# Attention and feed-forward on one core: the value products of two head pairs put into one TensorE step

## The chip, the cores and the metric

The kernel runs on one core of one Trainium2 chip. The metric is the device time of one execution in microseconds (us). Engines are named as the profile names them: PE is TensorE's matmuls, PEld its weight loads, DVE is VectorE, ACT is ScalarE, POOL is GpSimd, SP issues the DMAs. [...]

## What is computed

Attention over a window of 128 keys and 4 sink keys, for 4 sequences of 768 tokens with 8 heads of 64, and then a feed-forward product with a squared ReLU:

```python
keep = is_sink | in_window
scores = np.where(keep, scale * q @ k.T, -1e9)
a = np.exp(scores - max(scores))
a = a / (sum(a) + 1e-9)
x = a @ v                          # put together as 3072 tokens x 512
out = np.maximum(x @ w_in, 0) ** 2 @ w_out    # w_in 512 x 2048, w_out 2048 x 512
```

All is float32. The products of the feed-forward part are made exact enough by splitting both factors into a high and a low part, so that each product takes three matmuls.

## The kernel before

The 3072 tokens are eight chunks of 384 (half a sequence each). A chunk's attention goes by four head pairs (two heads of 64 fill the 128 partitions), so there are 32 pair steps `s` in all. A chunk's feed-forward part goes over 16 slices `fc` of 128 of the 2048 columns. For each slice PE makes the first product (line 837, 12 matmuls of 384 columns), ACT takes ReLU and square (850, 854), DVE makes the exact square's low part (859, 866), and one slice later PE makes the second product (882, 9 matmuls of 512 columns).

One pair of attention goes through these steps, from the third chunk on (`s >= 8`):

- scores on PE (521), two matmuls over KS and QS, which hold high and low parts that ACT, DVE or POOL have made (388, 478, 484, 489);
- mask and maximum on DVE (498), exponential on ACT (504), sum's reciprocal on DVE (562), and scaling of P by it, on POOL (569; in the first two chunks also on DVE, or on ACT in line 567);
- P is turned by DVE in blocks of 32 x 32 into T (727, 731); four DMAs put T into `via` in DRAM (744) and one DMA gets it back as PT with whole columns turned (757);
- the four sink columns of P are copied into the tile PSK in a high part (585) and a low part (583), both by POOL. DVE turns PSK into SKT (647), four small DMAs gather it (653), and ACT or DVE copies it to SK (388);
- the value step on PE: for each block of keys and each head a matmul of 64 columns of v against PT (785), which uses half of the array's columns, both heads side by side; then one matmul over the full array for the sinks (789). ACT and DVE then split the sum into x's high and low part (801, 806).

In the first two chunks (`turned`) PE itself turns P (698) and the sink columns (630), and scores are made from kn and qn with 64 rows of the array (515).

Which instruction stands where in each engine's queue is decided before the program runs, by the class `Plan`. Each step has a rank, the engines that may do it with an assumed cost, and the cells that it reads and writes. `Plan.order` picks step by step the one that could start first by these costs. Its numbers are the planner's, not the chip's. Three of its rules matter here: a step marked "port" (an SBUF pass of DVE or POOL) is not put beside another such pass of the other engine; a POOL step without that mark waits for `SHARE` of the running DVE pass; and a change of PE's mode (0: the full array, 1: 64 rows, 2: 64 columns) is priced at 0.2 each time. All engines then work through their queues in order.

In SBUF, many tiles share a place: PT is one buffer for all pairs, T is one buffer for both heads of a pair, PSK has two, and the ReLU's result r has two (G0 and G1). Three PSUM banks ("att") serve scores and value sums from the second chunk on.

Of the kernel before, what the change touches and what calls it, by code (L numbers as in the profile page):

```python
# [18 lines left out]
P = 128  # L19
D = 64  # L20
NS = 4
# [12 lines left out]
SHARE = 0.5  # L34
# [4 lines left out]
SC_DVE = 0.3  # L39
CLAIM = (True, False)  # L40
KS_ACT = 0.0
URGE = 0.5
LOW_DVE = 0.0
CP_DVE = 0.3
SC_ACT = 0.3
# [8 lines left out]
def f32(ap):  # L54
    return ap.bitcast(F32)


class Plan:
# [45 lines left out]
    def order(self):  # L104
# [3 lines left out]
        while open_:  # L108
# [16 lines left out]
            for e, able in best.items():  # L125
# [5 lines left out]
                if chosen is None or a[0] < chosen[1][0] or (e == "POOL" and a[0] <= chosen[1][0] + 0.001):  # L131
                    chosen = e, a
# [37 lines left out]
def sink_window_attention_moe(  # L170
# [25 lines left out]
    with ExitStack() as fast:  # L196
# [18 lines left out]
        ident = wp.tile([P, P], F32, name="ident")  # L215
# [39 lines left out]
        either = sb("G1", [P, P], F32, "either")  # L255
# [16 lines left out]
        PSK = [wp.tile([P, NQ, 32], F32R, name=f"PSK{i}") for i in range(2)]  # L272
# [3 lines left out]
        for t in (VS, PSKW, *PSK, *SK):  # L276
            nc.gpsimd.memset(f32(t), 0.0)
# [6 lines left out]
        PT = wp.tile([P, 4, 2 * NQ, 2, 32], F32, name="PT")  # L284
        PT_flat = PT.rearrange("p r i h b -> p (r i h b)")
# [126 lines left out]
        def attention(s, rank):  # L412
# [36 lines left out]
            if plain:  # L449
                which = (0, 1, 2, 0, 2, 0, 2, 0)[s]  # L450
                if which == 1:
                    both = lambda: sb("T", [P, 2, NQ, BAND], F32, f"P_{s}")
# [121 lines left out]
            psk = PSK[two]  # L574
            psk_cell = ("PSK", two)
            if turned:
                psk = PSKW[:, two]

            def part_sinks(h, low):
                src = Pt(h)[:, i0:NQ, P:BS]  # L580
                to = psk[:, i0:NQ, 0 : 6 * NS].rearrange("p q (t c) -> p q t c", c=2 * NS)[..., h * NS : h * NS + NS]
                if low:
                    nc.gpsimd.tensor_tensor(to[:, :, 1], src, f32(to[:, :, 0]), op=ALU.subtract)
                else:
                    nc.gpsimd.tensor_copy(to[:, :, 0:3:2], src.unsqueeze(2).broadcast_to([P, NQ - i0, 2, NS]))  # L585

            groups = ((0, 1),) if plain else ((0,), (1,))
            for heads in groups:
# [10 lines left out]
                for h in heads:  # L599
                    for i in range(NQ):  # L600
# [12 lines left out]
                        ("POOL", 0.2), r - URGE + 0.01, lambda h=h: part_sinks(h, False),  # L613
# [3 lines left out]
                        ("POOL", 0.2), r - URGE + 0.01, lambda h=h: part_sinks(h, True),  # L617
# [8 lines left out]
            if turned:  # L626

                def turn_sinks():
# [5 lines left out]
                    ("PE", 0.11 * (NQ - i0), 0), r, turn_sinks, reads=own_sinks + [("spare", 23)], writes=[key], take=[("any" if early else "att", key)],  # L634
# [9 lines left out]
            else:  # L644
# [13 lines left out]
                for x in range(4):  # L658
# [3 lines left out]
                add(  # L662
                    [("ACT", 0.4), ("DVE", 0.35, "port", CP_DVE)], rank(0.8) - URGE,
                    lambda e: copy(e, sk[0:32, :, i0:NQ], rows_()[0:32, :, i0:NQ]),
                    reads=VR, writes=[sk_cell],
                )
# [3 lines left out]
            if turned:  # L670
# [6 lines left out]
                for bi, members in enumerate(parts):  # L677
# [15 lines left out]
                    def turn(blocks=blocks, key_t=key_t):  # L693
# [12 lines left out]
                        reads=[(P_cell(h), i) for h in hs for i in range(NQ)] + [P_cell(h) for h in hs],  # L706
# [8 lines left out]
            else:  # L715
                T = lambda: sb("T", [P, 4, 2 * NQ, 2, 32], F32, f"T_{s}")
                used = 2 * NQ - i0

                def turn(h, which):
                    if which == 0:  # L720
                        dst, src = T()[:, :, 0:NQ, h], Pt(h)[:, :, BS:BAND]
                    elif which == 1:
                        dst, src = T()[:, :, NQ : 2 * NQ - 1, h], Pt(h)[:, 1:NQ, 0:P]
                    else:
                        dst, src = T()[:, :, 2 * NQ - 1, h], Pt(h)[:, 0, 0:P]
# [6 lines left out]

                for h in range(2):
                    r = rank(1.3 if not plain and h == 0 else 0.9)
                    for which in range(3 - i0):
                        add(
                            ("DVE", (0.49, 0.33, 0.2)[which]), r - URGE, lambda h=h, which=which: turn(h, which),
                            reads=[(P_cell(h), i) for i in range(NQ)] + [P_cell(h)] + ["T"] * (h + which > 0),
                            writes=[("T", h, which)] + ["T", ("TP", 0), ("TP", 1)] * (h + which == 0),
                        )  # L740
                via = lambda: dram(f"via{s % 2}", [4, 32, 4, 2 * NQ, 2, 32], f"via_{s}")

                def put(r):
                    nc.sync.dma_start(
                        out=via()[:, :, r, 0:used].rearrange("c a i h b -> a c (i h b)"),
# [473 lines left out]
```

## Time and profile before

| | |
|---|---|
| median of the runs shown | 678.01 us (676.47, 678.01 and 1077.74) |
| the profiled execution's own time | 677.97 us |
| its span, first to last instruction | 676.2 us |
| granted TensorE clock over the span | 0.994 |
| DMA | 104.91 MB in 62547 packets, mean 155 GB/s |

The span is what the views show; 1.8 us of the execution's time lie outside of it. In the views, a row "L785 PE MATMUL bank<-PT,vn" is the matmul of line 785 that reads PT and v and writes a bank; "x12" counts its records (a float32 matmul in the 64-column form leaves two). The chain of work goes back from the last instruction to what released it, so that its pieces fill the span without gaps: the length of a PE piece there is the time until the next piece, not the time for which one matmul is under way. Behind an arrow stands what ended an engine's idle time.

### The profile page before, as it was taken

The page shows a single profiled execution, that of the slowest core. Times are in us where ns is not written, and L with a number is a line of the kernel's source. Part 1 is how long each engine was busy: PE and PEld are TensorE (multiplying, and loading weights), DVE is VectorE, ACT ScalarE, POOL GpSimd, SP SyncE. Part 2 cuts the span into 40 slices and gives each one's busy share as a digit, 9 for nine tenths or more (in the row PEclk, how much of TensorE's full clock was granted, in tenths as well). Part 3 has the DMA queues.
Part 4 walks back from the last instruction along what each step waited for, and adds up shares of the span by engine and source line. Part 5 has one row for each costly group of instructions (what it writes and reads, how often), then busy time and mean ns, then how long its engine had stood idle before and what let it go on. Part 6 is the DMA issues. An engine that isn't in the chain of part 4 may idle for free.

```text
span 676.2 us, 11302 instructions
## 1 busy us (share of the span) xinstructions
PE 658.2 (97%) x3662; PEld 573.3 (85%) x3662; DVE 445.5 (66%) x1211; ACT 392.5 (58%) x1142; POOL 125.2 (19%) x319
## 2 busy tenths in 40 slices
PE   4999999999999999999999999999999999999996
PEld 3767889998888888898888888888889888899985
DVE  7899999878877656575667756665666664242221
ACT  5898644367665445566666676666677665542221
POOL 4542200033242221111112211111121221000000
PEclk9899999999999999999999999999999999999999
DMA  7856665025977544366555856557556853310001
GB/s 235 261 155 187 208 207 177 32 75 165 263 200 205 165 120 121 109 209 198 176 158 170 243 168 192 175 164 200 164 157 187 245 169 118 115 62 1 1 0 52
DMA packets 62547, 104.91 MB, mean 155 GB/s; under 512 B 10800, under 2 KB 39216, under 8 KB 62480
## 3 DMA queue, kind: packets, MB, share of 16 engines
q1 hardware_dynamic: 62480, 104.11, 51.8%
q8 instruction: 31, 0.51, 0.3%
q14 instruction: 36, 0.29, 0.1%
HBM read 78.72 MB, written 24.38 MB: 152 GB/s over the span
## 4 chain that ended last, share of the span: by engine, by line
PE 89%; DVE 7%; POOL 1%; issue 1%; DMA 1%; ACT 0%; SPq 0%; DVEq 0%; POOLq 0%
PE bank L882 39%; PE bank L837 38%; PE bank L785 5%; PE bank L521 5%; DVE P L498 2%; PE bank L789 1%; DVE w L350 1%; DVE f L333 1%; DVE f L340 1%; DVE f L326 1%; DVE P L569 1%; DMA kn<-in_k_dram 1%; POOL PSK_wide L585 1%; DVE gl L866 0%; PE bank L515 0%
## 5 line engine op out<-in xcount | busy, mean ns | idle before, releaser
L837 PE MATMUL bank<-x,w 128*128 128x384 f32 x1536 | 301.2, 338 | 0.0
L837 PEld LDWEIGHTS bank<-x,w 128*128 128x128 f32 x1536 | 266.1, 188 | 8.3 <-issue 1.4
L882 PE MATMUL bank<-w,gh 128*128 128x512 f32 x768 | 242.6, 397 | 0.0
L569 POOL TENSOR_SCALAR P<-P,small 128x260 f32<-128x260 f32 (+1 forms) x168 | 83.4, 513 | 415.6 <-DVE small L562 401.2
L882 PEld LDWEIGHTS bank<-w,gh 128*128 128x128 f32 x768 | 138.7, 188 | 22.4 <-issue 1.0
L882 PE MATMUL bank<-w,gl 128*128 128x512 f32 x384 | 151.8, 395 | 0.0
L850 ACT ACTIVATE r<-bank 128x384 f32<-128x384 f32 x128 | 62.7, 490 | 114.1 <-PE bank L837 112.8
L504 ACT ACTIVATE P<-P,nbs 128x260 f32<-128x260 f32 (+1 forms) x192 | 93.6, 488 | 60.3 <-DVE nbs L498 57.9
L859 DVE TENSOR_TENSOR bank<-bank,r 128x384 f32<-128x384 f32 x128 | 72.0, 563 | 77.4 <-ACT r L850 76.8
L498 DVE CUSTOM_DVE_ANT_0 P<-bank,maskA 128x260 f32<-128x260 f32 x128 | 53.1, 421 | 53.4 <-PE bank L521 52.8
L882 PEld LDWEIGHTS bank<-w,gl 128*128 128x128 f32 x384 | 72.1, 188 | 16.9
L866 DVE TENSOR_TENSOR gl<-bank,gh 128x384 fp32r<-128x384 f32 x128 | 71.1, 556 | 19.1 <-ACT gh L854 10.1
L854 ACT ACTIVATE gh<-r 128x384 fp32r<-128x384 f32 x128 | 66.7, 521 | 2.8 <-PE bank L882 0.7
L727 DVE STREAM_TRANSPOSE T<-P 128x384 f32<-128x384 f32 x96 | 45.3, 494 | 24.8 <-POOL P L569 24.7
L521 PEld LDWEIGHTS bank<-KS,QS 128*128 128x128 f32 x288 | 52.0, 188 | 5.7
L521 PE MATMUL bank<-KS,QS 128*128 128x260 f32 (+1 forms) x288 | 54.8, 277 | 0.0
L785 PE MATMUL bank<-PT,vn 128*64 128x256 f32 (+1 forms) x392 | 40.6, 347 | 0.0
L801 ACT CAST x<-bank 128x384 fp32r<-128x384 f32 x32 | 15.2, 474 | 42.1 <-PE bank L789 42.1
L785 PEld LDWEIGHTS bank<-PT,vn 128*64 128x64 f32 x392 | 25.7, 139 | 15.7 <-issue 6.3
L504 ACT ACTIVATION_READ_ACCUMULATOR P<-P,nbs 128x1 f32 x192 | 36.0, 188 | 0.0
L498 DVE CUSTOM_DVE_ANT_0 P<-bank,mask 128x128 f32<-128x128 f32 (+1 forms) x64 | 22.0, 353 | 19.3 <-PE bank L521 19.0
L374 ACT ACTIVATE sq<-sq,theta 128x256 bf16<-128x256 bf16 x64 | 32.2, 503 | 1.1
(99 smaller groups left out, 518.4 us busy)
## 6 DMA issues: line engine op xcount, KB each, us to landing
raw<-in_moe_w_dram SPq DMA_DIRECT2D x32, 512.0 KB, 4.0
half<-in_moe_w_dram SPq DMA_DIRECT2D x64, 256.0 KB, 3.9
via<-T SPq DMA_DIRECT2D x48, 192.0 KB, 3.1
PT<-via SPq DMA_DIRECT2D x12, 768.0 KB, 4.8
via<-T SPq DMA_DIRECT2D x48, 160.0 KB, 2.7
PT<-via SPq DMA_DIRECT2D x12, 640.0 KB, 5.4
kn<-in_k_dram SPq DMA_DIRECT2D x24, 264.0 KB, 3.9
qn<-in_q_dram SPq DMA_DIRECT2D x32, 192.0 KB, 3.7
```

The source lines that it names most:

```text
L498: nc.vector.tensor_tensor_reduce(Pt(h)[:, i, o : o + n], ps_[:, 0:n], mask[:, 0:n], -SCALE, BIG, ALU.add, ALU.min, nb)
L504: nc.scalar.activation(Pt(h)[:, i, o : o + n], Pt(h)[:, i, o : o + n], AF.Exp, bias=nb, scale=-1.0, accum_out=sm[:, h, i : i + 1],)
L521: nc.tensor.matmul(bank(key)[:, 0:n], QS(h)[:, cols], flat[:, a, c0 : c0 + n], start=(a == 0), stop=(a == 1),)
L569: {"POOL": nc.gpsimd, "DVE": nc.vector}[engine].tensor_scalar(a, a, rs[:, h, i : i + 1], 1.0, op0=ALU.mult, op1=ALU.mult)
L727: nc.vector.transpose(dst.rearrange("p c j b -> p j c b"), src.rearrange("p j (c b) -> p j c b", b=32))
L785: nc.tensor.matmul(xo[h * D : h * D + D, qs[0] * P : qs[0] * P + len(qs) * P], vn[:, kk, h, :], rhs(), start=(n == 0), stop=False, skip_gr ...
L837: nc.tensor.matmul(bank(key)[:, 0:TOK], wi[fc][:, i, cc * P : (cc + 1) * P], xt[:, cc, :], start=(cc == 0 and j == 0), stop=(cc == NCC - 1 ...
L850: lambda key=key, r=r: nc.scalar.activation(r(), bank(key)[:, 0:TOK], AF.Relu),
L854: ("ACT", 0.41), n - 9, lambda gh=gh, r=r: nc.scalar.activation(gh(), r(), AF.Square),
L859: lambda key=key, r=r: nc.vector.tensor_tensor(bank(key)[:, 0:TOK], bank(key)[:, 0:TOK], r(), op=ALU.mult),
L866: lambda key=key, gh=gh, gl=gl: nc.vector.tensor_tensor(gl(), bank(key)[:, 0:TOK], f32(gh()), op=ALU.subtract),
L882: nc.tensor.matmul(bank(okey), gt()[:, ts_], wo[f][:, i, :], start=(f == f0 and j == 0), stop=(f == f1 - 1 and j == 2),)
```

## The change

From the third chunk on, the value matmuls of an even pair no longer make a step of their own. They wait for those of the odd pair behind it, and one PE step holds both pairs' value matmuls and the even pair's sink matmul. The odd pair's copy to SK is put behind that step (there is one SK buffer), and its sink matmul is a second, short step:

```diff
+            if turned:
+                add(
+                    ("PE", spent + 0.2 + sunk, 2, 0), r, lambda: (values(), sink_values()),
+                    reads=[sk_cell, "VS"] + mine[2], writes=[key_x], take=[("any" if early else "att", key_x)],
+                )
+                parts(p, key_x, *xs[slot[c]])
+            elif p % 2 == 0:
+                waiting[0] = mine
+            else:
+                first, first_sinks, cells, first_key = waiting[0]
+                add(
+                    ("PE", 2 * spent + 0.2 + sunk, 2, 0), r, lambda: (first(), values(), first_sinks()),
+                    reads=[sk_cell, "VS"] + cells + mine[2], writes=[first_key, key_x],
+                    take=[("att", first_key), ("att", key_x)],
+                )
+                take_sinks()
+                add(("PE", sunk, 0), r, sink_values, reads=[sk_cell, "VS"], writes=[key_x])
+                parts(p - 1, first_key, *xs[slot[c]])
+                parts(p, key_x, *xs[slot[c]])
```

For that, both pairs' turned P must be there at once. PT gets a second buffer for odd pairs (`PT2`), T holds one head, and the way through DRAM goes by head: eight puts and two gets a pair, each half as large.

```diff
-                T = lambda: sb("T", [P, 4, 2 * NQ, 2, 32], F32, f"T_{s}")
+                T = lambda h: sb("T", [P, 4, 2 * NQ, 32], F32, f"T_{s}_{h}")
...
+                PTs = PT if s % 2 == 0 else sb("PT2", [P, 2, 4, 2 * NQ, 32], F32, "PT_1")
...
+                    for x in range(4):
+                        add(
+                            ("SP", 0.42, 2.9, 90), rank(0.8 if h else 1.2), lambda h=h, x=x: put(h, x),
...
+                for h in range(2):
+                    add(
+                        ("SP", 0.42, 3.5, 360), rank(0.5 if h else 0.9), lambda h=h: get(h),
```

The room comes from smaller tiles: one PSK in place of two, one r (G0) in place of two, and `ident` shares a place with the scratch tile `sq` of the weight checks.

The planner's numbers change too: a POOL step without the "port" mark now waits for the whole of a running DVE pass, scaling of P in the first two chunks is given more readily to DVE and ACT, the copies of sink columns may go to DVE, and the third chunk's attention is due six slices earlier.

```diff
-SHARE = 0.5
+SHARE = 1.0
...
-SC_DVE = 0.3
+SC_DVE = 0.1
...
+SOON = 6
+PS_DVE = 0.2
...
-SC_ACT = 0.3
+SC_ACT = 0.1
...
-                if chosen is None or a[0] < chosen[1][0] or (e == "POOL" and a[0] <= chosen[1][0] + 0.001):
+                if chosen is None or a[0] < chosen[1][0]:
...
-                        ("POOL", 0.2), r - URGE + 0.01, lambda h=h: part_sinks(h, False),
+                        [("POOL", 0.2), ("DVE", 0.12, "port", PS_DVE)], r - URGE + 0.01, lambda e, h=h: part_sinks(e, h, False),
...
-                base, w = starts[nxt], (2.0 if nxt == 2 else 4.0)
+                base, w = starts[nxt] - (SOON if nxt == 2 else 0), (2.0 if nxt == 2 else 4.0)
```

Lines of the changed kernel are numbered higher: 785, 789 and 837 become 794, 800 and 868, 882 becomes 913, 350, 569, 583 and 585 become 352, 571, 582 and 584, and 698 becomes 701.

Three places show what that does to the queues. The first is PE in the fifth chunk's attention, before: a value step (785 with the sinks in 789) stands alone between products of the feed-forward part.

```order
L837 MATMUL bank_70<-x_146,w_317 128x384 x2
L837 MATMUL bank_70<-x_147,w_317 128x384
L785 MATMUL bank_69<-PT,vn_144 64x256 x4
L785 MATMUL bank_69<-PT,vn_144 64x128 x2
L789 MATMUL bank_69<-SK_128,VS 128x256
L837 MATMUL bank_70<-x_146,w_317 128x384 x2
L837 MATMUL bank_70<-x_147,w_317 128x384
```

And now, PE in the same chunk (PT_148 is the second buffer, bank_69 the odd pair's sum):

```order
L868 MATMUL bank_70<-x_145,w_708 128x384
L794 MATMUL bank_67<-PT,vn_142 64x256 x4
L794 MATMUL bank_67<-PT,vn_142 64x128 x2
L794 MATMUL bank_69<-PT_148,vn_143 64x256 x4
L794 MATMUL bank_69<-PT_148,vn_143 64x128 x2
L800 MATMUL bank_67<-SK_127,VS 128x256
L913 MATMUL bank_72<-w_703,gh_587 128x512 x2
L913 MATMUL bank_72<-w_703,gl_596 128x512
L913 MATMUL bank_73<-w_703,gh_587 128x512 x2
L913 MATMUL bank_73<-w_703,gl_596 128x512
L800 MATMUL bank_69<-SK_127,VS 128x256
```

Two pairs' value matmuls follow each other, and the odd pair's sink matmul stands four rows behind the even pair's. This is so twelve times.

The second place is the first pair of the first chunk, on DVE, before (f is a weight row in the making, VS the sinks' values):

```order
L569 TENSOR_SCALAR P_1_185<-P_1_185,small 128x260
L401 CAST VS<-vs_169 24x512
L406 SCALAR_TENSOR_TENSOR VS<-VS,third,vs_169 24x512
L326 TENSOR_SCALAR f_268<-raw_171 128x512
L326 TENSOR_SCALAR f_272<-raw_175 128x512
L333 SCALAR_TENSOR_TENSOR f_268<-raw_171,f_268 128x512
L333 SCALAR_TENSOR_TENSOR f_272<-raw_175,f_272 128x512
L340 SCALAR_TENSOR_TENSOR f_268<-raw_171,f_268 128x512
L562 RECIPROCAL small<-small 128x6
```

And now, on DVE:

```order
L571 TENSOR_SCALAR P_1_184<-P_1_184,small 128x260
L403 CAST VS<-vs_168 24x512
L584 CAST PSK_wide<-P_0_178 128x2x2x4
L582 TENSOR_TENSOR PSK_wide<-P_0_178,PSK_wide 128x2x4
L408 SCALAR_TENSOR_TENSOR VS<-VS,third,vs_168 24x512
L328 TENSOR_SCALAR f_266<-raw_170 128x512
L328 TENSOR_SCALAR f_269<-raw_174 128x512
L335 SCALAR_TENSOR_TENSOR f_266<-raw_170,f_266 128x512
L564 RECIPROCAL small<-small 128x6
```

DVE has taken over the sink columns of the first head, and the second pair's reciprocal stands behind one weight pass of line 335 in place of three (333, 333, 340). POOL keeps the second head's two copies. On ACT the step that feeds this reciprocal (593, now 592) stood behind the copy of the first pair's sinks to SK, and now stands five rows ahead of it.

The third place is DVE's last weight row. Before, it was row 318 of 2027, among other weight passes:

```order
L333 SCALAR_TENSOR_TENSOR f_1404<-raw_1344,f_1404 128x512
L401 CAST VS<-vs_347 24x512
L340 SCALAR_TENSOR_TENSOR f_1404<-raw_1344,f_1404 128x512
L406 SCALAR_TENSOR_TENSOR VS<-VS,third,vs_347 24x512
L859 TENSOR_TENSOR bank_71<-bank_71,r_583 128x384
L350 TENSOR_TENSOR w_1444<-f_1404,w_1444 128x512
```

Now, on DVE, it is row 405 of 2025:

```order
L730 STREAM_TRANSPOSE T_0_1760<-P_0_1604 128x3x4x32
L897 TENSOR_TENSOR gl_596<-bank_71,gh_587 128x384
L730 STREAM_TRANSPOSE T_0_1760<-P_0_1604 128x2x4x32
L564 RECIPROCAL small<-small 128x3
L342 SCALAR_TENSOR_TENSOR f_1718<-raw_1459,f_1718 128x512
L500 ISA P_0_1788,nbs<-bank_67,mask_86 128x128
L500 ISA nbs 128x1
L352 TENSOR_TENSOR w_1786<-f_1718,w_1786 128x512
```

The third chunk's scores, transposes and reciprocals have moved ahead of the last weight rows, 87 rows in all.

More of the change, by code (lines that the diff above doesn't have):

```diff
@@ L573, in attention, with part_sinks @@
             two = s % 2
[L574 to L579, printed above, removed]
+            psk, psk_cell = (PSKW[:, two], ("PSKW", two)) if turned else (PSK, ("PSK", 0))
+            def part_sinks(e, h, low):
                 src = Pt(h)[:, i0:NQ, P:BS]
@@ L661, in attention, with take_sinks @@
                     )
[L662 to L666, printed above, removed]
+                def take_sinks():
+                    add(
+                        [("ACT", 0.4), ("DVE", 0.35, "port", CP_DVE)], rank(0.8) - URGE,
+                        lambda e: copy(e, sk[0:32, :, i0:NQ], rows_()[0:32, :, i0:NQ]),
+                        reads=VR, writes=[sk_cell],
+                    )
+                if not p % 2:
+                    take_sinks()
             todo = ([], [])
@@ L731, in turn, with put, get @@
                         nc.vector.transpose(dst, src.rearrange("p (c b) -> p c b", b=32))
+                via = lambda: dram(f"via{s % 2}", [2, 4, 32, 4, 2 * NQ, 32], f"via_{s}")
+                PTs = PT if s % 2 == 0 else sb("PT2", [P, 2, 4, 2 * NQ, 32], F32, "PT_1")
+                PT_cells = [("PT", x) for x in range(3)] if s % 2 == 0 else [("TP", x) for x in range(2)]
+                def put(h, r):
+                    nc.sync.dma_start(
+                        out=via()[h, :, :, r, 0:used].rearrange("c a i b -> a c (i b)"),
+                        in_=T(h)[32 * r : 32 * r + 32, :, 0:used].rearrange("a c i b -> a c (i b)"),
+                    )
+                def get(h):
+                    nc.sync.dma_start(
+                        out=PTs[:, h, :, 0:used].rearrange("p r i b -> p r (i b)"),
+                        in_=via()[h, :, :, :, 0:used].rearrange("c a r i b -> (c a) r (i b)"),
+                    )
                 for h in range(2):
-                    r = rank(1.3 if not plain and h == 0 else 0.9)
+                    r = rank(0.9 if h else 1.3)
                     for which in range(3 - i0):
@@ L737, in attention @@
                             ("DVE", (0.49, 0.33, 0.2)[which]), r - URGE, lambda h=h, which=which: turn(h, which),
-                            reads=[(P_cell(h), i) for i in range(NQ)] + [P_cell(h)] + ["T"] * (h + which > 0),
-                            writes=[("T", h, which)] + ["T", ("TP", 0), ("TP", 1)] * (h + which == 0),
-                        )
[L741 to L745, printed above, removed]
-                        in_=T()[32 * r : 32 * r + 32, :, 0:used].rearrange("a c i h b -> a c (i h b)"),
-                    )
@@ L799, in attention @@
-            xh, xl = xs[slot[c]]
-            add(
-                ("ACT", 0.4), r - URGE, lambda: nc.scalar.copy(xh[:, p, :], bank(key_x)[:, 0:TOK]),
-                reads=[key_x], writes=[("xh", slot[c], p)],
-            )
-            add(
-                ("DVE", 0.47), r - URGE,
-                lambda: nc.vector.tensor_tensor(xl[:, p, :], bank(key_x)[:, 0:TOK], f32(xh[:, p, :]), op=ALU.subtract),
-                reads=[key_x, ("xh", slot[c], p)], writes=[("xl", slot[c], p)], drop=[key_x],
-            )
+            spent, sunk = (1.07 if half == 0 else 1.28), (0.175 if i0 == 0 else 0.12)
@@ new lines, in parts @@
+            def parts(p, key_x, xh, xl):
+                add(
+                    ("ACT", 0.4), r - URGE, lambda: nc.scalar.copy(xh[:, p, :], bank(key_x)[:, 0:TOK]),
+                    reads=[key_x], writes=[("xh", slot[c], p)],
+                )
+                add(
+                    ("DVE", 0.47), r - URGE,
+                    lambda: nc.vector.tensor_tensor(xl[:, p, :], bank(key_x)[:, 0:TOK], f32(xh[:, p, :]), op=ALU.subtract),
+                    reads=[key_x, ("xh", slot[c], p)], writes=[("xl", slot[c], p)], drop=[key_x],
+                )
@@ L810, in sink_window_attention_moe @@
+        waiting = [None]
+        todo_cells = {}
         todo_cells = {}
```

77 lines of the change are left out of this document (36 added, 41 removed).

## The prediction

> **What bounds the kernel now.** I read the page's busy shares first, then busy time by stage, then the chain of work that ended last, and then the start engine by engine. The page's first part:
>
> ```profile
> PE 658.2 (97%) x3662; PEld 573.3 (85%) x3662; DVE 445.5 (66%) x1211; ACT 392.5 (58%) x1142; POOL 125.2 (19%) x319
> ```
>
> PE is busy almost always. By stage (stretch, its length, then busy us of PE, PEld, DVE, ACT, POOL, granted clock, DMA share, GB/s):
>
> ```profile
> 0.00:18.00 18.00, 8.13 (x47) 6.27 (x48) 13.79 (x65) 9.87 (x36) 9.01 (x25) 0.94 0.77 238
> 18.00:75.00 57.00, 55.62 (x355) 41.27 (x355) 54.92 (x151) 48.64 (x141) 24.23 (x51) 0.96 0.66 203
> 75.00:130.00 55.00, 54.97 (x288) 49.24 (x289) 53.47 (x101) 25.36 (x48) 0.00 (x0) 1.00 0.50 161
> 130.00:200.00 70.00, 70.00 (x397) 62.00 (x398) 55.45 (x168) 44.92 (x134) 21.43 (x53) 1.00 0.59 164
> 200.00:585.00 385.00, 385.00 (x2158) 339.12 (x2155) 241.08 (x669) 237.30 (x724) 70.53 (x191) 1.00 0.59 173
> ```
>
> From 18 us on PE hardly stands: 1.4 us to 75 us, nothing from 75 to 585. So two things can make the kernel shorter: less PE work behind 18 us, or a shorter start. The other engines' busy time counts only where PE comes to wait for them. DVE, full until 130 us, is the candidate.
>
> **What a value step costs.** The chain of work gives each PE piece's own share of the time. Two value steps, one of the first half of a sequence (640 columns a head, 256 sink columns) and one of the second (768 and 384):
>
> ```profile
> 343.92 1.59 PE bank L837 x9
> 345.50 1.23 PE bank L785 x12
> 346.74 0.32 PE bank L789
> 347.05 0.54 PE bank L837 x3
> ...
> 365.30 1.45 PE bank L785 x16
> 366.75 0.37 PE bank L789
> ```
>
> 128 columns a head more make 1.45 - 1.23 = 0.22 us. Five such parts are 1.10, so 0.13 of the 1.23 us is for going into the half-array form. For the sinks 128 columns more make 0.05 to 0.06; twice that is 0.12, so 0.20 of the 0.32 us is for going back. A visit to this form costs 0.33 us beside its work.
>
> **The change, part by part.**
>
> *Twelve visits fewer.* 24 value steps become 12, and the matmuls stay the same: 12 x 0.33 = 4.0 us less on PE, in a stage in which PE never stands. This is the main term. It is 0 if what I call the visit's cost is paid for each bank or each pair, and it could not be above 4.0 by these rows.
>
> *The odd pair's sinks.* Its matmul waits for a copy to SK, which waits for the even pair's sink matmul. As cover, the order shows mostly three first-product and three second-product matmuls, beside that sink matmul's own slot:
>
> ```profile
> 346.67 0.39 PE L789 MATMUL bank<-SK,VS 128*128 128x256 f32 x1
> 376.99 2.11 PE bank L882 x9
> 379.34 2.10 PE bank L837 x12
> L388 ACT CAST SK<-sk 32x384 fp32r<-32x384 f32 x3 | 1.5, 512 | 1.3 <-PE bank L789 1.3
> ```
>
> That is 2.11 / 3 + 2.10 / 4 = 1.23 us, and some 0.2 us for the slot, against 0.39 (matmul) + 0.51 (copy) = 0.90 us and two hand-offs. It is hidden if ACT is free. ACT is busy 237 of 385 us, so it is often in another pass of about half a microsecond, and some steps will wait a little. Bounds: 0, and 12 x 0.5 = 6 us. I take 0.3 in all, since 0.5 us of cover remain, as long as one such pass.
>
> *T by heads.* DVE's transposes of a pair's second head wait until the first head's four puts have left T. Order puts 7 to 24 DVE rows between them; at 241.08 / 669 = 0.36 us each that is 2.5 to 8.6 us. Landing times by size:
>
> ```profile
> via<-T SPq DMA_DIRECT2D x48, 192.0 KB, 3.1
> via<-T SPq DMA_DIRECT2D x48, 160.0 KB, 2.7
> sk<-SKT SPq DMA_DIRECT2D x48, 8.0 KB, 3.0
> ...
> 350.02 2.27 SPq L744 DMA_DIRECT2D via<-T  x4
> ```
>
> Size hardly matters to the landing, so a half-size put saves little: 2.27 + 3 makes some 5 us, and DVE may stand for 2.5 us where only 7 rows lie between. Queued behind are the passes of 859 and 866. The product that needs them starts one second and one first product after its first product's end, 2.11 + 2.10 = 4.2 us:
>
> ```profile
> L850 ACT ACTIVATE r<-bank 128x384 f32<-128x384 f32 x128 | 62.7, 490 | 114.1 <-PE bank L837 112.8
> L859 DVE TENSOR_TENSOR bank<-bank,r 128x384 f32<-128x384 f32 x128 | 72.0, 563 | 77.4 <-ACT r L850 76.8
> L866 DVE TENSOR_TENSOR gl<-bank,gh 128x384 fp32r<-128x384 f32 x128 | 71.1, 556 | 19.1 <-ACT gh L854 10.1
> ```
>
> They take 0.49 + 0.56 + 0.56 = 1.6 us, so a stand of up to 2.6 us is hidden: 0. The single r buffer is hidden by the same 2.6 us. The 120 DMAs more take 0.57 us of SP each (2.27 / 4), five a pair of some 20 us. PE waits for no get today; 0, and 12 x 0.57 = 7 us if one more issue lay ahead of each step. I take 0, since the even pair's get is now needed only with the odd pair's.
>
> *The start.* The first value step is late because the sink columns are. POOL, then PE, ACT and DVE around 15 us:
>
> ```profile
> 14.97 2.53 POOL L585 CAST PSK_wide<-P 128x16 fp32r<-128x16 f32 x1
> 17.57 0.20 POOL L583 TENSOR_TENSOR PSK_wide<-P,PSK_wide 128x8 fp32r<-128x8 f32 x1
> ...
> 17.83 0.69 PE L630 MATMUL bank<-ident,PSK_wide 128*128 128x128 f32 x2 [3.10 <-POOL PSK_wide L583]
> 18.45 2.40 PE L785 MATMUL bank<-PT,vn 128*64 128x128 f32 x12
> ...
> 18.61 0.36 ACT L388 CAST SK<-bank 32x256 fp32r<-32x256 f32 x1 [3.01 <-PE bank L630]
> ...
> 14.88 0.75 DVE L326 TENSOR_SCALAR f<-raw 128x512 int32<-128x512 int32 x2
> 15.56 1.27 DVE L333 SCALAR_TENSOR_TENSOR f<-raw,f 128x512 int32<-128x512 int32 x2
> 16.76 0.67 DVE L340 SCALAR_TENSOR_TENSOR f<-raw,f 128x512 int32<-128x512 int32 x1
> 19.21 0.19 DVE L562 RECIPROCAL small<-small 128x6 f32<-128x6 f32 x1 [1.77 <-ACT small L593]
> ```
>
> [...] PE stands 3.10 us, ACT 3.01 for PE, and DVE 1.77 for ACT. In the new order two of the four sink passes are on DVE ahead of the weight passes, and the second pair's reciprocal no longer queues behind the copy to SK. But PE now has a turn of the second pair, which needs that reciprocal, ahead of the first value step. So PE's wait changes its reason more than its length. What goes is DVE's 1.77 us; against it stand three sink passes on DVE, 0.6 us. I take -1.2 us. Best case: the whole 3.10 us goes, and so does the half clock behind it:
>
> ```profile
> 16.00:18.00 2.00, 0.17 (x1) 0.17 (x2) 1.43 (x3) 0.00 (x0) 1.69 (x2) 0.50 1.06 330
> 20.00:22.00 2.00, 2.00 (x10) 1.48 (x9) 1.69 (x5) 1.66 (x8) 2.00 (x4) 0.50 0.39 105
> 22.00:24.00 2.00, 2.00 (x18) 1.73 (x16) 1.95 (x5) 2.00 (x6) 1.89 (x5) 0.80 0.88 238
> ```
>
> PE did the 4.5 us from 18.45 us to about 22.9 at half clock, so 2.2 us more: -5.3 in all. Worst case: by the order, DVE has three sink passes, four scalings and two copies to PT more in the first two chunks, and one low pass less. Their prices, beside 0.20 for a sink pass:
>
> ```profile
> L569 DVE TENSOR_SCALAR P<-P,small 128x260 f32<-128x260 f32 x14 | 6.4, 465 | 0.0
> L388 ACT COPY PT<-bank 128x512 f32<-128x512 f32 x10 | 5.6, 570 | 0.0
> L350 DVE TENSOR_TENSOR w<-f,w 128x512 fp32r<-128x512 f32 x32 | 22.8, 716 | 0.1
> ```
>
> 0.6 + 1.9 + 1.1 - 0.7 = 2.9 us, if all of it came through to PE. The value taken lies nearer to none, as DVE's saved wait is the nearest row.
>
> [...]
>
> *One 64-row visit more in the start* (order: 14 entries in place of 13): 0 to 0.33 by the value step; I take 0.2.
>
> *The third chunk earlier.* 87 DVE rows come ahead of the last weight row. In the stage of the third chunk's attention a row takes 55.45 / 168 = 0.33 us, so that is 29 us. The row is ready, and first used, at:
>
> ```profile
> L350 DVE TENSOR_TENSOR w<-f,w x32: 669/682/1415, 22.6 to 130.5; 128x512 fp32r<-128x512 f32 x32
> ...
> 162.66 0.69 PE bank L882 x3
> ```
>
> 131 + 29 = 160 us, and the use, at 163, moves back by the third chunk's scores that are now ahead of it (26 rows of the order, some 3 us). So it is hidden by a margin of about 6 us: 0, and beyond that, the fourth rival.
>
> **The sum**, against the profiled execution's 677.97 us (the median of the runs, 678.01, is the same): -4.0 + 0.3 - 1.2 + 0.2 = -4.7, so 673.3 us.
>
> **Rivals.**
> - *Merging saves nothing*, as the cost is per bank: 677.97 + 0.3 - 1.2 + 0.2 = 677.3. The equal rest of 0.13 and 0.20 in both forms speaks for a cost per visit.
> - *The odd pair's sinks are late* at each of 12 steps by a full ACT pass, 0.5 us: 673.3 + 5.7 = 679.0. ACT's 62% speaks for some of it, the cover of 0.5 us against.
> - *The start is cured*: -5.3 in place of -1.2, 669.2 us. For it: DVE takes half of the sinks. Against: the turn that now stands ahead.
> - *Weights come late; slower than before.* In the stretch from 70 us on DVE keeps 130 to 200 us's share, 55.45 / 70 = 0.79, not 53.47 / 55 = 0.97. Until the last weight row it has 61 x 0.97 + 29 = 88 us of work; at 0.79 that ends at 70 + 111 = 181 us, 15 us after the use at 166. PE works its queue in order and stands, and the clock halves as above (2): 673.3 + 17 = 690.3. It decides from a share under 88 / 96 = 0.92. Against: the weight passes need no other engine and fill DVE's gaps.
>
> **How the numbers follow.** Chances: 0.53 for the forecast (own range 671 to 676), 0.08 no saving, 0.13 late sinks, 0.14 cured start, 0.10 late weights, 0.02 something else. The range 668.5 to 680.0 holds the forecast, the first three rivals mostly, not the fourth. Faster by over 2% would be under 664.4 us; no case gets there, and 0.03 is for what no row shows. Slower by over 2%, above 691.5, is the worse part of the fourth rival, 0.04. Within 2%, which is about what a measurement of this kernel can tell from no change: 0.93.
>
> **What would show it.** In the chain of the changed kernel: two value runs with no gap in twelve places, with one 0.13 and one 0.20 a pair of pairs; a second sink piece of 0.12 or 0.17 us with PE not waiting for ACT; at the start PE's first value step ahead of 18.45 us; no PE wait for a weight pass from 130 to 170 us. The forecast is wrong if PE shows waits from 75 to 585 us, or if the sums over value pieces do not fall by 4 us.

## The result, and the profile after

The changed kernel takes 670.82 us (median of 670.7 to 671.21 in four runs) against 678.21 us for the kernel before: a ratio of 0.9897, with a 95% interval of 0.9882 to 0.9912. That is 7.4 us less by the medians, 7.0 by the ratio, within 2%. The kernel before took 676.47, 678.01, 678.41 and 1077.74 us, and the ratio leaves the last, slow execution out. The prediction said 673.3 us, with a range of 668.5 to 680.0. The profiled execution took 670.76 us, its span is 669.0 us, its granted clock 0.995, and its DMAs went in 84438 packets (62547 before).

Busy time by stage of the changed kernel, in the same stretches as before (length, then busy us of PE, PEld, DVE, ACT, POOL, granted clock, DMA share, GB/s):

```profile
0.00:18.00 18.00, 9.72 (x54) 7.39 (x56) 14.29 (x70) 12.10 (x43) 6.64 (x24) 0.98 0.78 239
18.00:75.00 57.00, 56.71 (x362) 41.94 (x361) 56.14 (x158) 48.95 (x140) 17.63 (x41) 0.98 0.69 207
75.00:130.00 55.00, 54.41 (x294) 48.87 (x293) 53.56 (x119) 29.08 (x68) 7.96 (x13) 1.00 0.59 181
130.00:200.00 70.00, 70.00 (x399) 62.48 (x398) 55.13 (x153) 40.41 (x114) 18.82 (x44) 1.00 0.62 159
200.00:585.00 385.00, 385.00 (x2174) 342.94 (x2173) 238.86 (x659) 242.75 (x747) 67.94 (x185) 1.00 0.62 171
```

From 130 to 585 us PE still never stands, as before, so what is gained there is work that PE no longer has. Up to 130 us PE is busy for 9.72 + 56.71 + 54.41 = 120.84 us where it was 8.13 + 55.62 + 54.97 = 118.72, and the clock is higher (0.98 for 0.94 and 0.96). So the first 130 us now hold more of PE's work: 2.1 us by busy time, and some 3.5 us (an estimate) if each stretch's busy time is multiplied by its clock. It is not all gain: in the third stretch PE does 0.56 us less.

The chain of work of the changed kernel around two merged steps, one of the first half of a sequence and one of the second (start, length and records of each piece):

```profile
156.47 2.31 PE bank L794 x24
158.78 0.32 PE bank L800
159.10 0.17 PE bank L523 x2
...
160.63 0.12 PE bank L800
...
222.00 2.75 PE bank L794 x32
224.75 0.37 PE bank L800
...
226.35 0.18 PE bank L800
```

Before, two pairs took 2 x (1.23 + 0.32) = 3.10 us; now 2.31 + 0.32 + 0.12 = 2.75. In the second half it was 2 x (1.45 + 0.37) = 3.64, and is 2.75 + 0.37 + 0.18 = 3.30. So 0.35 and 0.34 us a pair of pairs are gone, 6 x 0.35 + 6 x 0.34 = 4.1 us in all. The other 3.3 us come from the first 130 us.

The start of the changed kernel, PE and then POOL, with PE's one stand behind 75 us as the last row:

```profile
14.62 0.42 PE L629 MATMUL bank<-ident,PSK_wide 128*128 128x128 f32 x2
16.87 0.96 PE L701 MATMUL bank<-ident,P 128*128 128x128 f32 x4 [1.83 <-DVE P L571]
17.76 2.40 PE L794 MATMUL bank<-PT,vn 128*64 128x128 f32 x12
...
23.36 1.30 PE L794 MATMUL bank<-PTS,vn 128*64 128x128 f32 x12
...
13.98 0.26 POOL L584 CAST PSK_wide<-P 128x16 fp32r<-128x16 f32 x1
...
99.69 0.50 PE L913 MATMUL bank<-w,gh 128*128 128x512 f32 x1 [0.59 <-DVE ob L955]
```

The first pair's sinks reach PE at 14.62 us in place of 17.83, POOL's copy takes 0.26 us in place of 2.53, and PE stands 1.83 us for the second pair's scaling by DVE in place of 3.10 for POOL. The second pair's value step starts at 23.36 us; before, it was 24.23. A stand of 0.59 us at 99 us is new: PE waits for DVE to copy output rows out of a bank.

### The profile page after: what moved, and what is told of

Its sections match the earlier page's. It is cut to its first block, busy times and chain, and to the rows that moved or that the text cites. A ratio compares the mean times of both kernels' runs of the same rounds, so it can differ in the third digit from the quotient of the medians.

```text
span 669.0 us, 11585 instructions
## 1 busy us (share of the span) xinstructions
PE 653.3 (98%) x3662; PEld 572.9 (86%) x3662; DVE 442.0 (66%) x1210; ACT 395.2 (59%) x1156; POOL 119.0 (18%) x305
## 2 busy tenths in 40 slices
DMA packets 84438, 104.95 MB, mean 157 GB/s; under 512 B 12720, under 2 KB 59568, under 8 KB 84368
## 4 chain that ended last, share of the span: by engine, by line
PE 87%; DVE 11%; issue 1%; DMA 1%; ACT 0%; SPq 0%; DVEq 0%
PE bank L913 37%; PE bank L868 37%; PE bank L794 5%; PE bank L523 5%; DVE f L335 2%; DVE P L500 2%; DVE w L352 1%; DVE f L342 1%; DVE f L328 1%; PE bank L800 1%; PE bank L517 1%; DVE gl L897 1%; DVE bank L890 1%; DVE P L571 1%; DMA kn<-in_k_dram 1%
## 5 line engine op out<-in xcount | busy, mean ns | idle before, releaser
L571 POOL TENSOR_SCALAR P<-P,small 128x260 f32<-128x260 f32 (+1 forms) x159 | 81.6, 529 | 417.5 <-DVE small L564 417.5
L794 PE MATMUL bank<-PT,vn 128*64 128x256 f32 (+1 forms) x392 | 38.0, 344 | 0.0
L369 ACT ACTIVATE sq<-half 128x256 bf16<-128x256 f32 x64 | 27.3, 427 | 6.3 <-DMA half<-in_moe_w_dram 5.9
```

Source lines behind the costliest of these rows:

```text
L571: {"POOL": nc.gpsimd, "DVE": nc.vector}[engine].tensor_scalar(a, a, rs[:, h, i : i + 1], 1.0, op0=ALU.mult, op1=ALU.mult)
L794: nc.tensor.matmul(xo[h * D : h * D + D, qs[0] * P : qs[0] * P + len(qs) * P], vn[:, kk, h, :], rhs(), start=(n == 0), stop=False, skip_gr ...
```

## The experiments

Every kernel was timed beside the kernel before (678.2 to 678.4 us in each set of runs):

| kernel | median us | ratio to before, 95% |
|---|---|---|
| the changed kernel | 670.82 | 0.9897 (0.9882 to 0.9912) |
| 1 pairs not merged | 674.84 | 0.9953 (0.9940 to 0.9967) |
| 2 merging alone, old numbers of the planner | 686.02 | 1.0117 (1.0099 to 1.0135) |
| 3 merged step with two visits | 674.91 | 0.9954 (0.9941 to 0.9968) |
| 4 third chunk at its old place | 683.93 | 1.0088 (1.0074 to 1.0103) |
| 5 not merged, third chunk at its old place | 678.88 | 1.0018 (1.0004 to 1.0031) |
| 6 third chunk ahead by 3, not 6 | 673.24 | 0.9938 (0.9919 to 0.9957) |
| 7 PE kept busy at 15 us | 670.51 | 0.9893 (0.9875 to 0.9910) |
| 8 sink passes on POOL alone | 675.12 | 0.9957 (0.9941 to 0.9973) |
| 9 first pair's sink passes on POOL, same order | 670.05 | 0.9881 (0.9866 to 0.9896) |
| 10 kernel before, third chunk ahead by 6 | 680.90 | 1.0040 (1.0027 to 1.0054) |
| 11 old numbers, but sink passes by either | 673.34 | 0.9934 (0.9921 to 0.9948) |
| 12 second chunk merged too, PE kept busy | 670.58 | 0.9887 (0.9872 to 0.9902) |

### What a visit costs: 1 and 3

Experiment 1 puts each pair's value step back by itself and keeps all else:

```diff
-                if not p % 2:
-                    take_sinks()
+                take_sinks()
...
-            if turned:
+            if True:
```

> The changed kernel with each pair's value step put back by itself (its heads, its sinks, and only then the next pair), all else as changed: T by heads, halved puts and gets, the second PT buffer, the planner's numbers, the earlier third chunk. If a visit to the half-array form costs 0.33 to 0.35 us and the twelve visits fewer are what the middle of the kernel gained, this is 4.0 to 4.2 us slower than the changed kernel: about 675.0 us, 0.995 of before, and the excess is back at the entries and exits of the value steps. If the gain came from the halved DMAs, the second buffer or T by heads, it stays at 671, 0.990 of before.

Experiment 3 only moves the even pair's sink matmul between the two pairs' value matmuls:

```diff
-                    ("PE", 2 * spent + 0.2 + sunk, 2, 0), r, lambda: (first(), values(), first_sinks()),
+                    ("PE", 2 * spent + 0.2 + sunk, 2, 0), r, lambda: (first(), first_sinks(), values()),
```

> The changed kernel with one thing moved: the even pair's sink matmul stands between the two pairs' value matmuls, not behind both. Same instructions, same waits, same DMAs, but 24 visits to the half-array form in place of 12. If the cost is one of visits, it is 12 x 0.35 = 4.2 us slower than the changed kernel, about 675.0 us (0.995 of before), and each merged step shows 0.13 more going in and 0.20 more going back. If the cost is per bank, or if the gain came from buffers, it stays at 671 us (0.990 of before).

Both are slower than the changed kernel by 4.0 and 4.1 us (3.8 and 3.9 by the ratios). In experiment 3 nothing else differs: the same instructions, buffers and DMAs. Its chain of work shows where the time is:

```profile
156.32 1.23 PE bank L794 x12
157.55 0.32 PE bank L800
157.87 1.23 PE bank L794 x12
159.10 0.37 PE bank L523 x2
...
160.81 0.12 PE bank L800
```

The second 1.23 is followed by two scores in the full array, which show 0.37 us where the same two show 0.17 us at 159.10 in the changed kernel. The first products behind it pay the same elsewhere: three of them show 0.73 us at 189.65 us, in place of 0.53. So the way back costs its 0.20 us whether sinks, scores or first products come next, and the way in shows in the two 1.23 (2.46 against 2.31, so 0.15). 1.23 + 0.32 + 1.23 + 0.20 + 0.12 = 3.10 us, as before the change. The cost belongs to the visit, and not to banks, pairs or buffers.

### What the earlier third chunk is for: 2, 4, 5, 6 and 10

Experiment 4 is the changed kernel with one number changed, and experiment 6 makes that number 3:

```diff
-SOON = 6
+SOON = 0
```

> The changed kernel with the third chunk's attention at its old place in the planner's ranks (SOON 0 in place of 6). The changed kernel shows a stand of PE of 0.76 us at 98.8 us, where a second product waits for a DVE copy of out rows. If the earlier third chunk is what made DVE late there, that stand goes and the time falls by 0.5 to 1 us, to about 670.0 us (0.988 of before). If the earlier third chunk is what keeps PE fed later, new waits come between 130 and 200 us and it is slower, 672 us or more (0.991).

> The changed kernel with the third chunk moved ahead by 3 in the ranks in place of 6. Six moved the second merged step from 205.1 to 186.6 us, so three should put its data at about 204 us in place of 213, against about 202 us at which PE ran out of other work. By that, a stand of 0 to 3 us with some half clock behind: 671 to 677 us. If the stand at 98.8 us goes (0.76 us) and none comes at 200, it is about 670.2 us (0.988).

Experiment 2 has all of the planner's numbers as before:

```diff
-SHARE = 1.0
+SHARE = 0.5
...
-SC_DVE = 0.1
+SC_DVE = 0.3
...
-SOON = 6
-PS_DVE = 0.2
+SOON = 0
+PS_DVE = 100.0
...
-SC_ACT = 0.1
+SC_ACT = 0.3
...
-                if chosen is None or a[0] < chosen[1][0]:
+                if chosen is None or a[0] < chosen[1][0] or (e == "POOL" and a[0] <= chosen[1][0] + 0.001):
```

> The changed kernel with the planner's numbers of before (shares, prices of scaling, the tie rule for POOL, sink passes on POOL alone, the third chunk at its old place), so the merging and its buffers alone. If the gain is 4.2 us of visits and 2.5 us of start, this is about 674 us, 0.994 of before, with the start as before: first value step near 18.45 us and about 6.8 us at half clock behind it. If the start's gain came with the moved buffers and not with the numbers, it is about 671.5 us, 0.990 of before. If merging saves nothing by itself, it is 678 us.

For experiments 2 and 4 no theory had 684 or 686 us in it. Experiment 4 is 13.1 us slower than the changed kernel, and the merging alone (experiment 2) is 7.7 us slower than the kernel before. PE of experiment 4 behind 200 us, and then two stretches of its busy time, with the granted clock behind POOL's share:

```profile
200.43 1.79 PE L523 MATMUL bank<-KS,QS 128*128 128x260 f32 x10
205.08 1.30 PE L794 MATMUL bank<-PT,vn 128*64 128x256 f32 x12 [2.86 <-DVE nbs L500]
211.35 2.40 PE L794 MATMUL bank<-PT,vn 128*64 128x256 f32 x12 [4.97 <-DMA PT<-via]
...
220.38 0.79 PE L868 MATMUL bank<-x,w 128*128 128x384 f32 x3 [1.31 <-DVE gl L897]
```

```profile
200.00:210.00 10.00, 3.47 (x26) 2.47 (x24) 5.77 (x22) 4.93 (x16) 1.91 (x6) 0.85 0.80 212
210.00:220.00 10.00, 7.65 (x32) 5.89 (x32) 6.55 (x18) 4.79 (x14) 2.25 (x5) 0.63 0.65 193
```

This is the third chunk's second merged step. PE has nothing else left when it comes, stands 2.86 us ahead of the third pair's matmuls, and then 4.97 us within the step, until the fourth pair's PT has come from DRAM. The stands sum to 9.1 us. The clock is down behind the second: of 7.65 us at 0.63 some 2.8 us are lost (an estimate). (In the stretch ahead of 210 us it is 0.85, but the matmuls at 205.08 us take their usual 1.30 us.) Together that is 11.9 of the 13.1 us. The stand at 99 us, which was thought to come with the earlier third chunk, is there without it too (0.4 us); only experiments 2 and 11, with the planner's old numbers, don't have it.

The kernel before had room at that place. Its fourth value step of the third chunk has products of the chunk ahead on both sides, and the third chunk's own begin at 204.37 us:

```profile
198.41 1.20 PE L837 MATMUL bank<-x,w 128*128 128x384 f32 x6
199.54 1.30 PE L785 MATMUL bank<-PT,vn 128*64 128x256 f32 x12
...
204.37 2.25 PE L837 MATMUL bank<-x,w 128*128 128x384 f32 x12
```

Experiment 5 tells whether the merging or the new buffers use up that room. It is experiment 1 with `SOON = 0`:

> The changed kernel with each pair's value step by itself again and the third chunk's attention at its old place in the ranks. With merged steps the old place cost 13 us: PE stood 2.9, 5.0 and 1.3 us from 202 to 220 us, inside the third chunk's second merged step, and ran at half clock behind. If it is the merging that needs the earlier place (a merged step ties the third pair's values to the fourth pair's data, and PE has run out of other products by then), the unmerged kernel has no such stand and takes 674 to 675 us (0.994 to 0.995 of before). If T by heads, the halved DMAs or the buffers make the third chunk's attention late, the stand stays and it takes 684 to 688 us.

It lies between the two: 4.0 us slower than experiment 1, 5.1 us faster than experiment 4. Its PE at the same place:

```profile
206.57 1.30 PE L793 MATMUL bank<-PT,vn 128*64 128x256 f32 x12 [1.73 <-DVE KS L390]
...
208.76 1.57 PE L867 MATMUL bank<-x,w 128*128 128x384 f32 x6 [0.57 <-ACT x L809]
```

The fourth value step is at 206.57 us where the kernel before had it at 199.54. So the new way of turning (T by heads, twice as many DMAs, one buffer each for r and PSK) makes the third chunk's attention 7 us later by itself, and PE stands: 1.73, 0.57 and a third time 0.21 us, 2.5 of the 4.0 us. (The planner's numbers don't: with the old ones, in experiment 2, the second merged step is at 207.87 us, later still.) The merging then ties the third pair's values to the fourth pair's data and turns 4.0 us into 13.1. Which of the parts of the new way makes the 7 us was not tried, and where the rest of the 4.0 us goes was not settled.

Experiment 6 shows that half of the shift isn't enough. PE's second merged step is no longer late, but a stand is left:

```profile
218.10 0.73 PE L913 MATMUL bank<-w,gh 128*128 128x512 f32 x2 [1.73 <-DVE ob L948]
```

Experiment 10 gives the earlier place to the kernel before:

```diff
-                base, w = starts[nxt], (2.0 if nxt == 2 else 4.0)
+                base, w = starts[nxt] - (6 if nxt == 2 else 0), (2.0 if nxt == 2 else 4.0)
```

> The kernel before with one number of the change: the third chunk's attention moved ahead by 6 in the ranks. Its PE has no stand behind 30 us, so if the earlier third chunk only makes up for what the new buffers and the merged steps make late, this is worth nothing here: 677.5 to 679 us (1.000 of before). If the earlier place is a gain of its own, as large as the 4.0 us that it was worth in the unmerged kernel, it is 674.3 us (0.994).

Neither expectation has it: there it costs 2.6 us (its profiled execution, at 678.47 us, was the fastest of five, and shows a stand of 0.57 us for DVE at 147.80 us, in a stretch that DVE fills, busy for 19.11 of the 20 us from 130 us on).

That execution also shows that the same start can go two ways. Up to 77 us PE, DVE, ACT and POOL have the same instructions in the same order as in the kernel before. Yet POOL's sink copy, which took 2.53 us there, takes 0.39 us, and PE's first value step starts at 16.30 us in place of 18.45:

```profile
15.05 0.39 POOL L585 CAST PSK_wide<-P 128x16 fp32r<-128x16 f32 x1
...
16.30 1.30 PE L785 MATMUL bank<-PT,vn 128*64 128x128 f32 x12
```

The times of the kernel before fall apart by about as much: over all sets of runs, 1077.74 us aside, 35 took 677.3 to 679.2 us and five took 675.9 to 676.8. Whether the five are those without the long copy isn't known, since they have no profile.

So the earlier place is no gain of its own. It is a price of up to 2.6 us that buys back 4.0 us in the unmerged kernel and 13.1 in the merged one.

### Where the start's gain comes from: 7, 8, 9 and 11

Experiment 7 gives PE 14 transposes of the identity ahead of the second pair's first turn. Their results are overwritten:

```diff
-                    def turn(blocks=blocks, key_t=key_t):
+                    def turn(blocks=blocks, key_t=key_t, bi=bi):
+                        for _ in range(14 if s == 1 and bi == 0 else 0):
+                            nc.tensor.transpose(bank(key_t)[:, 0:P], ident, ident)
```

> The changed kernel with 14 transposes of the identity matrix in the queue of PE ahead of the second pair's first turn, into the bank that this turn then overwrites: 14 x 0.109 = 1.5 us of extra PE work in the 1.83 us in which PE stands at 15 to 16.9 us. If that stand is what brings the half clock from 17.3 to 20.7 us, the clock stays up and 3.4 / 2 = 1.7 us go: about 669.1 us (0.987 of before). If the clock falls for another reason, or if what PE does from 17 to 21 us waits for DVE and ACT anyway, it stays at 670.8 us (0.989).

Its PE from 15 us on, and then one stretch of its busy time:

```profile
15.01 1.69 PE L698 MATMUL bank<-ident 128*128 128x128 f32 x14
17.01 0.77 PE L703 MATMUL bank<-ident,P 128*128 128x128 f32 x4 [0.31 <-DVE P L571]
17.71 1.30 PE L796 MATMUL bank<-PT,vn 128*64 128x128 f32 x12
...
20.82 0.60 PE L517 MATMUL bank<-kn,qn 64*128 64x128 f32 x4 [0.58 <-DMA kn<-in_k_dram]
...
22.95 1.30 PE L796 MATMUL bank<-PTS,vn 128*64 128x128 f32 x12
```

```profile
18.00:20.00 2.00, 1.96 (x19) 1.34 (x15) 2.00 (x6) 2.00 (x7) 0.52 (x1) 1.00 0.91 189
```

The clock stays up (1.00 from 18 to 20 us, where the changed kernel has 0.50), and the first value step's matmuls take 1.30 us in place of 2.40. Yet the kernel gains 0.3 us, less than the runs scatter. The changed kernel's own runs say the same: the one with the highest clock over its span (0.999, the others 0.995 and 0.996) is the slowest of the four, at 671.21 us. In experiment 7 PE is done earlier and then waits for kn from DRAM, and the second pair's value step starts only 0.4 us earlier than 23.36. The half clock is real, but what it costs here is mostly hidden behind data that is not there.

Experiment 8 leaves the sink passes to POOL alone (`PS_DVE = 100.0`); experiment 11 leaves them to either, and has the other numbers of experiment 2, with `SOON` 6:

> The changed kernel with the passes over the sink columns on POOL alone, as before the change; the other numbers of the planner as changed. The order moves the second pair's first turn ahead of the first pair's sinks. If the start's 2.5 us came from moving two of these passes to DVE, away from POOL's 2.53 us copy, they are lost: about 673.3 us (0.993 of before), with one POOL sink copy of 2 us or more and half clock for longer than 3.4 us. If they came from the other numbers (the price of scaling, POOL behind DVE's passes), it stays at 671 us (0.990).

> The changed kernel with the planner's other numbers as before (its share of POOL's waiting, the prices of scaling on DVE and ACT, the tie rule for POOL), so that of the start's changes only the choice of DVE or POOL for the sink passes is left. The order then has the first value step ahead of the second pair's turns. If that choice is what the start gains by, this stays within 0.7 us of the changed kernel's 670.8 us (0.989 of before) and the first value step is at 18 us or earlier. If the other numbers are needed for it, the start is as before and it takes about 673.3 us (0.993).

Experiment 8 loses 4.3 us and experiment 11 2.5 us. So both parts are needed, with the orders that the planner makes of them. But the reason that was expected isn't what experiment 8 shows. Its order has the second pair's turns ahead of the first pair's sinks, no copy of POOL lasts 2 us (from 12 to 24 us two together took 0.58 or 0.60 us, single ones 0.20 and 0.52), and PE waits for DVE:

```profile
16.86 0.33 PE L701 MATMUL bank<-ident,P 128*128 128x128 f32 x1 [2.18 <-DVE P L571]
18.87 0.90 PE L701 MATMUL bank<-ident,P 128*128 128x128 f32 x3 [1.68 <-DVE P L571]
...
21.41 2.40 PE L794 MATMUL bank<-PT,vn 128*64 128x128 f32 x12
```

Experiment 11 has its first value step at 15.81 us, earlier than any other kernel here, and is slower all the same. The list of PE's waits from 12 to 75 us in experiment 11 (total us, times, longest), its first four rows of six:

```profile
PE bank L701 <- POOL P L571: 3.0, 5, 1.6
PE bank L629 <- POOL PSK_wide L582: 0.8, 1, 0.8
PE bank L629 <- DVE x L815: 0.6, 1, 0.6
PE bank L701 <- DVE nbs L500: 0.5, 1, 0.5
```

The old prices leave more of the scaling of P to POOL, and PE's turns wait for it, 3.0 us in five places; with the other rows PE's waits sum to 5.6 us. In the changed kernel they are 3.2 us for DVE's scaling and 0.2 us more, 3.4 us. So the time at which the first value step starts is not the measure of the start, and neither is the wait for P alone, which is as long in both. The sum of all PE's waits gives 2.2 of the 2.5 us. In experiment 8 it is 5.8 us, and the clock is at 0.50 from 18.1 to 24.9 us besides.

Experiment 9 keeps the changed kernel's order and issues the first pair's two DVE sink passes on POOL:

```diff
             def part_sinks(e, h, low):
+                e = "POOL" if s == 0 else e
```

> The changed kernel in the same order, but the first pair's two sink passes that stand on DVE (0.15 and 0.17 us at 14.1 to 14.5 us) are issued on POOL at their place, behind POOL's own two, where DVE runs its passes of 0.4 to 0.7 us without a gap. [...] If only the order matters, POOL's copy takes 0.2 to 0.5 us and the time stays at 670.8 us.

The two passes on POOL, and the first value step on PE:

```profile
13.88 0.19 POOL L585 CAST PSK_wide<-P 128x16 fp32r<-128x16 f32 x1
14.15 0.55 POOL L583 TENSOR_TENSOR PSK_wide<-P,PSK_wide 128x8 fp32r<-128x8 f32 x1
...
17.37 1.30 PE L795 MATMUL bank<-PT,vn 128*64 128x128 f32 x12
```

The expectation for a start in which only the order matters comes near: POOL's passes take 0.19 and 0.55 us, and the kernel isn't slower but 0.8 us faster. DVE has 0.32 us less to do and scales the second pair 0.2 us earlier, the clock stays at 1.00, and PE's first value step starts at 17.37 us. Its ratio and the changed kernel's overlap in their intervals, and the two were timed in different sets of runs, so this is the fastest version seen but not shown to be faster.

### One stage further: 12

Experiment 12 merges the second chunk's four value steps by pairs too, on top of experiment 7. Those pairs have two buffers for everything already:

```diff
-            if turned:
+            if early:
...
+                last = sink_values if turned else lambda: None
                 add(
-                    ("PE", 2 * spent + 0.2 + sunk, 2, 0), r, lambda: (first(), values(), first_sinks()),
+                    ("PE", 2 * spent + 0.2 + sunk, 2, 0), r, lambda: (first(), values(), first_sinks(), last()),
```

> The changed kernel with the 14 extra transposes at 15 us (0.3 us by their run) and with the second chunk's four value steps merged by pairs as well, which needs no new buffer, since these pairs alternate between two sets. If a visit costs the same there and PE is what bounds that stretch, two visits fewer save 2 x 0.33 = 0.7 us: about 669.8 us (0.988 of before). If DVE bounds the stretch from 18 to 130 us, where it is busy for 0.98 of the time, or if tying two pairs together makes PE wait, nothing is saved or time is lost: 670.5 us or more.

It takes 670.58 us, against 670.51 in experiment 7: no saving shows. By the ratios it is 0.4 us less, and the intervals are about 1 us to either side, so a saving of the expected 0.7 us is not excluded. The stand for DVE's output copy, at 99 us in the changed kernel, comes at another place:

```profile
175.54 0.73 PE L917 MATMUL bank<-w,gh 128*128 128x512 f32 x2 [0.46 <-DVE ob L959]
```

DVE is full to 130 us in this run too, busy for 56.36 of the 57 us from 18 us on and for 53.63 of the next 55, so that PE work saved ahead of it can come back as a wait for DVE. That this is all of it was not shown.

## Why the prediction was right, and where it was not

- *Twelve visits fewer, -4.0 us.* Right, and by its own reason. The rows give 4.1, undoing the merging 4.0, and doubling the visits alone 4.1. The rival that merging saves nothing is out.
- *The odd pair's sinks, +0.3 us.* It was 0: the second sink pieces are 0.12 and 0.18 us long, as asked for, and from 130 to 585 us PE waits for nothing. The cover of 1.23 us was enough each time. The rival of late sinks is out.
- *One 64-row visit more in the start, +0.2 us.* No run separates it from the rest of the start.
- *The start, -1.2 us.* Mis-sized: all that isn't merging came to -3.4 us (experiment 1 against before), where the prediction's other terms make -0.7. Its reason was also too narrow. It followed one POOL copy, one first value step and the half clock behind it. The clock was worth 0.3 us (experiment 7), and an earlier first value step nothing (experiment 11). What the runs show is that the gain goes when more of the scaling of P stays with POOL (experiment 11), or when the sink passes do, which changes the order too (experiment 8). Two sink passes put back on POOL in the same order cost nothing (experiment 9), so for them the order counts and not the engine. How the gain splits was not settled, and the stand that DVE's load brings at 99 us takes back 0.6 us. The long copy from which the working set out is not fixed by the order either: it took 0.39 us in experiment 10. The 0.20 us row behind it is the subtraction of line 583; the other head's copy took 0.38 us.
- *T by heads, 120 DMAs more, one buffer r: 0.* *The third chunk earlier: 0.* Their sum is 0 as forecast, but neither term is. This is where the prediction's working failed. The first was covered by "PE waits for no get today" and by 2.6 us of cover in the steady chunks; the third chunk has less, and with the new way of turning PE would have stood there, for 4.0 us unmerged and 13.1 merged. The second was costed as a move with a risk, weights that come late. The weights were not late (the last pass of line 352 on DVE starts at 152.7 us, where the working had 160), and the move is what pays for the first. That the two cancel is luck as far as the working goes, which has neither. The rival on the slower side named the wrong mechanism: the one that nearly happened is a merged step without its second pair.
- *"Size hardly matters to the landing."* Wrong in the rows of the changed kernel, from issue to landing, where 192 and 768 KB had taken 3.1 and 4.8 us:

```profile
via<-T SPq DMA_DIRECT2D x96, 96.0 KB, 2.0
PT<-via SPq DMA_DIRECT2D x24, 384.0 KB, 3.7
```

  It had been read from 8, 160 and 192 KB, different transfers under different load. No term rested on it, since T's wait was costed at 0.

- *The signs.* Most came as named: the first value step at 17.76 us, ahead of 18.45, twelve merged runs, second sink pieces as said, and no wait for a weight pass. But "waits from 75 to 585 us" were named as a sign that the forecast is wrong, and there is one, 0.59 us at 99 us. No term has it.
- *The rivals.* 670.82 us lies just below the forecast's own range of 671 to 676, and nearer to the cured start's 669.2 than to 673.3. But the start was not cured in that rival's way: of PE's 3.10 us 1.83 are left, and a half clock of 3.4 us behind them.

So the sum came within 2.5 us, with the large term right, all that isn't merging too small by 2.7 (against the median of before, 678.21), and two errors of 13 us that cancelled because the change was made with both parts together.

## What to carry to other kernels

In this kernel each change to the half-array form and back cost 0.13 to 0.15 us in and 0.20 out, so put work of the same form side by side; but a step that waits for two inputs is as late as the later one (PE stood 4.97 us within such a step in experiment 4), and needs its producers moved ahead by as much. When a change brings several parts, don't cost each against the kernel before: ask what each part would do without the others, above all where one of them looks useless. A saved wait or a restored clock counts only if the data behind it is there: the clock restored in experiment 7 gained 0.3 us. And a profile is one execution: the same order of instructions had its first value step at 18.45 us in one and at 16.30 us in another, so a single long instruction is a weak ground for a term.

## What the hardware showed that was not expected

- *The clock behind nearly the same stand.* PE's stand at 15 us was 1.83 to 1.87 us in the changed kernel and experiments 1, 3, 4, 5 and 6. The granted clock then fell to 0.50 in the changed kernel and in experiment 3, was 0.61 and 0.53 from 18 to 20 and from 20 to 22 us in experiment 6, and stayed at 1.00 in experiments 1, 4 and 5. So here a stand of 1.83 us was followed by the half clock, and one of 1.86 us was not. The half clock behind it lasted 3.41 us in the changed kernel, from 17.31 to 20.72 us; before the change it began within the stand of 3.10 us and lasted 6.83, from 15.98 to 22.81 us. What also differed is how long PE was busy around the stand. For the changed kernel the 3.41 us ahead of the half clock and the half clock itself, then for experiment 1 two such stretches around its stand (stretch, length, PE's busy time, granted clock, DMA share, GB/s):

```profile
13.90:17.31 3.41, 1.50 (x10) 1.00 1.00 355
17.31:20.72 3.41, 3.41 (x18) 0.50 0.94 214
...
12.39:15.81 3.42, 1.98 (x12) 1.00 0.99 365
15.81:19.22 3.41, 2.52 (x19) 1.00 1.08 278
```

  PE is busy for 1.50 us of the stretch ahead of the half clock in the changed kernel; in experiment 1 it is busy for 1.98 and 2.52 us, and the clock stays at 1.00. Experiments 6 and 7 differ in the same sense: PE is busy for 1.58 us from 15.03 to 18.45 us and the half clock follows in the one; for 3.10 us from 15.11 to 18.52 us, with the extra transposes, and the clock stays at 1.00 in the other. That PE's busy time is what decides was not shown.
- *POOL beside DVE.* The same 16-element sink copy took 0.19 us in experiment 9, 0.26 and 0.52 in the changed kernel and 2.53 before the change, all of them near gapless passes of DVE. Experiment 9 puts a subtraction of POOL beside such a chain too, at 0.55 us, and experiment 10 runs the very copy of 2.53 us, beside the same passes, in 0.39. So the 2.53 us is not what a chain of DVE passes brought each time. What made that one copy so long was not settled.
